# A sparse-attention and expert-attention kernel: half-size loads for batch 1, a converting load of the output weights, and a new order of all steps

## Chip, cores and metric

The kernel runs on one core of one Trainium2 chip. The metric is the device time of one execution in microseconds (us). The core has five engines that run their own queues in order: PE (matrix multiplications and transposes), DVE (vector), ACT (exponentials and copies), POOL (general, and the issuer of loads that convert types) and SP (issuer of plain loads and stores). They meet only at semaphores. The loads themselves are carried by 16 DMA engines.

## The reference

Two layers follow each other. The first is attention over q, k and v of 4 batches, 8 heads, 768 positions and 64 values: each query sees the keys closer than 16 positions, and beside them 24 summaries, one for each block of 32 positions (the maximum of its keys and the mean of its values).

```python
k_sum = k.reshape(B, H, nb, block, D).max(axis=3)
v_sum = v.reshape(B, H, nb, block, D).mean(axis=3)
scores_l = scale * q @ k.T            # kept where |i - j| < 16
scores_s = scale * q @ k_sum.T + log(block)
a = softmax(concat(scores_l, scores_s))
x = a @ concat(v, v_sum)              # heads side by side: 512 wide
```

The second is a mixture of four causal attention experts over x. A gate of four logits picks the best two experts of each position and weighs them by a softmax over the two; each expert has its own 512x64 matrices wq, wk, wv and a 64x512 matrix wo.

```python
for e in range(4):
    ye = causal_softmax((x@wq[e]) @ (x@wk[e]).T * scale) @ (x@wv[e]) @ wo[e]
    out += gate_weight[e] * ye        # zero where e is not among the two
```

## The kernel before

**Steps and the table.** The function `make_plan` defines 766 steps with `R.step`, and numbers them as they are defined. A step is a small piece of work for one engine, such as the 16 transposes that turn the keys of two heads. The text `TABLE` (lines 55 to 108) lists every step once as `number,engine,slots`: V is DVE, A is ACT, G is POOL, S is SP and P is PE; the slots say which buffer of its class each new tile takes. `Plan.emit` goes through it and calls the steps one by one. So each engine executes its steps strictly in the order of the table, and a step whose input is late holds up all that stands behind it on its engine.

**Names.** A step's name carries its batch, then its part. Heads go in pairs: `c` is 0 to 3, and two pairs form a group `g`. For batch 0, pair 1:

- `dk001`, `dq001` load keys and queries (lines 254 to 270; group 0, part 1). They are issued by POOL and convert fp32 to fp16 on the way. `load_qk` takes a number of parts: with 2 parts each load carries two heads, with 1 part four heads.
- `dv01` loads the values of the pair with four transfers on SP (lines 281 to 288), `hc01` copies the halo rows that neighbouring windows share (290 to 293), `bs01`, `be01` and `ds01` form the block means of the values (a product with the constant `sel`, an evacuation, a broadcast; 295 to 332). For the groups of batches 2 and 3 POOL adds up a tree instead (`dvs`, `tr`; 334 to 356).
- `tk01` and `tq01` transpose keys and queries on PE (372, 394). `tk` needs the constant `idr` (225), which is built from `id16`. `kw01`, `rk01`, `ksc01` and `cq01` evacuate them (376 to 401).
- `sc010`, `ex010`, `av010`: scores, exponential, product with the values, in two halves (406 to 442); they need the constants `mt` and `pi`. `rc`, `xm`, `tx`, `hi` and `lo` divide by the sum, transpose the result and split it into two fp16 parts (444 to 484).
- `weights` (486 to 537) loads the expert weights once, in fp32, into two spare `a2` buffers: `dw00` to `dw11` (wq and wk), `dwv0`, `dwv1`, `dwo`, all on SP. `cw`, `cvg` and `co` convert them to fp16.
- The second layer of a batch (539 to 751): `vp` (values and gate logits), `ga` to `gc` (gate), `pp` (projections), `sp` and `es` (scores and exponential of two experts, in six units), `dm` (causal mask on POOL), `aw` (products), `r2` and `wv` (weighting), `tw` and `ct` (transpose), `op` (product with wo, line 737), `oc` (evacuation) and `od` (store).
- `vone`, `id16`, `id32`, `idr`, `kwz`, `mt`, `pi`, `sel`, `knz`, `vtz`, `v2o`, `w1m`, `at`, `zz` build constants and clear paddings. `fl0` to `fl23` are products of a zero tile into unused banks; those marked P are executed, those marked A do nothing.

PE works on the second layer of one batch between the pieces of the first layer of the next. A single buffer `vt` serves the trees, six buffers `vb` the values, three each the keys and the queries, and seven rows `ob` the output.

**Order at the places that the prediction speaks of.** At the start POOL executes dk001, dk000, vone2, kwz, dq000, dq001, dq010, id16, idr, vone0, dq011, dk011, sel, ksc01, mt, hc00; ACT executes dwg, hc01, kw01, cq01, ds01, ex010, cq00, ksc00, ex011; PE executes tk01, bs01, tq01, tk00, tq00, sc010, bs00, sc011. Around the first use of wo PE executes sc200, tw000, sc201, sc211, tw010, pp101, sp115, sp114, tk22, tk23, sp111, op00, vp10.

The steps are executed by these lines, and the function whose loads change is this:

```python
for i, eng, slots in table:
    st = self.steps[i]
    ...
    st.fn(eng)
...
def load_qk(b, g, parts):
    n = 4 // parts
    ...
    R.step(f"dk{b}{g}{i}", {"G": 0.72}, [], [kn[b, g]], gk, dma=n * 96 * 0.098 / 16)
```

Of the kernel before, what the change touches and what calls it, by code (L numbers as in the profile page):

```python
# [15 lines left out]
S = 768  # L16
# [11 lines left out]
QP = 128  # L28
TREE = {(2, 0), (2, 1), (3, 0), (3, 1)}
# [31 lines left out]
233,G,2 252,P,6.1.1 83,V, 125,G, 111,P,4.4 84,V, 253,A, 0,G, 63,P,7.1 144,S,0 112,A, 128,P,0.5 64,V, 130,P,2.1 129,A,
143,S, 102,P,4.0.0 254,V, 131,A, 142,S,1 65,G, 113,P,0.0 269,P,7.0.2 103,V, 141,S, 132,P,2.0.2 270,A, 242,G,0 140,S,
104,V, 114,A, 145,S, 237,G, 271,V, 133,P, 85,P,4.1.1 235,G, 134,V, 135,V, 115,P,0.1.0 86,A, 116,P, 1,A, 87,V, 45,G,
136,P,6.2.2 117,V, 273,P,2.1 118,V, 137,A, 307,P,3.2 238,P,4.0 272,A, 138,V, 274,A, 150,G, 308,A, 275,P,0.2 239,V,
46,G, 119,P,6.3.3 276,A, 244,S,0 277,P,2.3 286,P,5.2.0 120,A, 240,G, 256,P,4.0 287,V, 278,A, 196,P,0.0 255,A, 241,G,
257,A, 288,V, 194,P,2.1 246,S,2 197,A, 121,V, 289,G, 149,G, 303,P,4.0.2 195,A, 290,P,5.1 304,V, 260,P,0.5 147,A,
204,P,6.0 408,S,0 279,P,2.0.1 406,S, 261,A, 305,V, 409,S, 280,P, 245,G, 205,A, 407,S, 152,P,0.0.0 402,S,3 281,V,
282,V, 291,A, 258,P,6.1 154,A, 283,P,4.4.4 259,A, 247,G, 153,V, 201,P,2 284,V, 202,A, 146,S, 306,G, 248,P,0.1 285,V,
401,G,1 203,G, 210,P,6 249,V, 198,P,2 263,P,4.1.2 199,A, 262,P, 251,G, 211,A, 165,P,0.2 404,S,4 264,V, 265,V, 415,G,2
213,P,2 292,P,6.4 410,G, 166,V, 214,A, 266,P,4.5.5 293,A, 311,P,2.0 267,V, 294,P,0.2 312,A, 158,P,6 295,A, 268,V,  # L70
400,G,1 309,P,2.3 250,G, 160,V, 207,P,0 310,A, 155,P,4 159,V, 208,A, 411,G,0 167,P,6.0 156,V, 157,V, 161,V,2.0 162,A,
163,V, 314,P,0.0.0 168,A, 313,P, 151,A, 164,V, 209,G, 585,S,0 172,P,4.1 200,G, 315,V, 169,P,6 582,S, 173,A, 316,V,
212,G, 297,P,2.1.1 584,S, 206,G, 583,S, 296,P, 170,A, 174,G, 413,G, 181,P,0 416,S,0 298,V, 317,P,4.6.6 299,V, 182,A,
449,P,6.0 432,P,7.1 318,V, 215,G, 450,A, 300,P,2.7.7 403,G, 178,P,0 433,A, 319,V, 445,P,6.1.1 418,S,5 179,A,
428,P,7.2.0 301,V, 184,P,4 414,G,1 185,A, 175,P,0 302,V, 364,P,4.1 183,G, 176,A, 171,G, 447,V, 180,G, 177,G, 362,P,2.0
365,A, 430,V, 186,G, 586,G, 446,A, 429,V, 216,P,0.0.0 218,P, 363,A, 188,P,1.1.4 217,P, 369,P,6.0 576,G,0 219,V,
375,P,2 448,A, 370,A, 189,P, 220,V, 431,G, 587,G,1 187,P, 376,A, 366,P,6 190,V, 323,P,0.1.1 367,A, 191,V, 434,P,2.5
324,V, 325,V, 192,P,4.0 436,P,6.1 435,A, 412,G, 193,V, 420,S,0 453,P,0.0 423,S, 221,P,2.1 454,A, 422,S, 335,P,4.2
222,V, 421,S, 437,A, 368,G, 578,S,2 377,G, 405,G, 381,P,0 372,P,2 336,V, 382,A, 462,P,6.0.2 373,A, 479,P,7.2.1 464,V,
378,P,0 223,P,4.0 379,A, 374,G, 320,P,2 480,A, 224,V, 380,G, 577,G,0 451,P,0.3 321,V, 383,G, 481,V, 225,S, 326,P,4  # L80
452,A, 419,G, 322,V, 463,A, 333,P,0.0 327,V, 371,G, 329,V,7.1 328,A, 424,G, 331,V, 330,A, 229,P,2.2 334,A, 332,V,
226,P,4.4 230,A, 590,G,1 346,P,0.1 227,V, 343,P,6 347,A, 386,P,1.0.2 425,G,0 384,P, 344,A, 228,S, 385,P, 337,P,4
387,V, 604,P,0.1.0 338,A, 388,V, 349,P,6 466,P,1.2 350,A, 606,V, 352,P,4 427,G, 456,P,2.0.2 597,S,0 353,A, 467,V,
340,P,6 389,P,4.0 341,A, 455,P, 390,V, 345,G, 348,G, 483,P,1.1 605,A, 592,S,4 354,G, 457,V, 439,P,4.1.0 458,V, 465,G,
351,G, 438,P, 484,A, 339,G, 38,G,1 482,A, 468,P,6.2 440,V, 470,P,2.4 441,V, 469,A, 625,P,0.0 621,P,1.0.2 471,A, 626,V,
342,G, 487,P,6.0 580,S,1 426,G, 459,P,4.0.0 488,A, 622,V, 485,P,2.3 608,P,0.2 486,A, 355,P,0.1.6 607,G, 623,V, 357,P,
609,A, 593,G, 594,S,3 356,P, 460,A, 612,P,2.1 358,V, 489,P,0.0.1 417,G, 359,V, 613,A, 490,P, 461,V, 588,G, 360,P,2.1
# [71 lines left out]
def make_plan(nc, T, q, k, v, moe_w_gate, moe_wq, moe_wk, moe_wv, moe_wo, out):  # L159
# [3 lines left out]
    def en(e):  # L163
        return getattr(nc, ENG[e])
# [109 lines left out]
    def load_v(b, c):  # L274
# [83 lines left out]
    def stage1_pair(b, c, hs, ls):  # L358
# [122 lines left out]
        def loc(e):  # L481
            nc.vector.tensor_tensor(turned(T["lo"][lo.slot]), xpv(),  # L482
                                    turned(T["hi"][hi.slot]), AL.subtract)
        R.step(f"lo{b}{c}", {"V": 0.96}, [xp, hi], [lo], loc)

    def weights():
        sA, sB = R.buf("a2"), R.buf("a2")
        wg32, wgt = st("wg32"), st("wgt")
        pw, pv, po = [st("pw0"), st("pw1")], st("pv"), st("po")
# [412 lines left out]
```

## Time and profile before

| what | value |
|---|---|
| time, median of 3 runs | 161.74 us (161.12 to 162.04) |
| time of the profiled execution | 162.94 us |
| span in its trace | 161.2 us |
| granted PE clock | 1.0 throughout |
| moved by DMA | 24.57 MB, mean 152 GB/s |
| read from and written to memory | 24.13 MB, 6.29 MB |

The page counts the busy time of each engine over the span, then cuts the span into 40 slices of 4.03 us, in which a digit is the busy share in tenths. A row of a timeline gives the start and the length of a run of like instructions, the engine, the line, the tiles (output, arrow, inputs) and, in brackets, how long the engine stood idle before it and what released it. Busy time of PE counts the length of instructions that overlap; two starts tell more than one length.

### The profile page before, as it was taken

How to read it: one execution, taken by the hardware profiler on the slowest of the kernel's cores; microseconds unless marked ns; L12 is line 12 of the kernel's file. 1: busy time of each engine (PE TensorE's matmuls, PEld its weight loads, DVE VectorE, ACT ScalarE, POOL GpSimd, SP SyncE). 2: the span in 40 equal slices, each digit the busy share in tenths (PEclk: the TensorE clock that was granted, in tenths of full speed). 3: DMA queues.
4: the chain of work that ended last, by engine and by line, in shares of the span. 5: the costliest groups of instructions: out<-in, count | busy, mean ns of one | idle time of the engine just before them, and what ended most of it. 6: DMA issues, size and time to landing. Idle time of an engine off the chain costs nothing.

```text
span 161.2 us, 6956 instructions
## 1 busy us (share of the span) xinstructions
PE 143.5 (89%) x2992; PEld 107.1 (66%) x2992; DVE 116.8 (72%) x236; ACT 119.5 (74%) x152; POOL 109.9 (68%) x184
## 2 busy tenths in 40 slices
PE   0049998769999999999999999998999998999994
PEld 0137796758687778577666988656778795466741
DVE  5527488985878967977786899968888578247940
ACT  0096999566996779898889997639788894999460
POOL 6987595984874999999999989649996230216100
PEclk9999999999999999999999999999999999999999
DMA  3999999997889996998799985699200000030746
GB/s 21 215 226 237 188 161 232 222 218 166 173 170 186 237 157 151 176 168 129 181 173 166 266 151 119 188 268 267 81 0 4 4 6 0 4 130 0 257 167 231
DMA packets 44158, 24.57 MB, mean 152 GB/s; under 512 B 33120, under 2 KB 40544, under 8 KB 43744
## 3 DMA queue, kind: packets, MB, share of 16 engines
q1 hardware_dynamic: 35552, 16.91, 43.7%
q0 software_dynamic: 7488, 6.29, 28.0%
q10 hardware_dynamic: 1088, 0.93, 1.7%
q8 instruction: 23, 0.38, 1.0%
q14 instruction: 7, 0.06, 0.1%
HBM read 24.13 MB, written 6.29 MB: 189 GB/s over the span
## 4 chain that ended last, share of the span: by engine, by line
PE 69%; ACT 12%; POOL 5%; issue 4%; DMA 4%; SPq 2%; DVE 2%; POOLq 0%; ACTq 0%; DVEq 0%
PE ps L437 13%; PE ps L630 12%; PE ps L554 6%; PE ps L678 6%; PE ps L654 6%; PE ps L366 6%; PE ps L737 4%; DMA out_dram<-ob 4%; PE ps L304 4%; PE ps L414 3%; PE ps L463 3%; ACT a L662 3%; PE ps L420 3%; ACT aT L427 2%; ACT kw L168 2%
## 5 line engine op out<-in xcount | busy, mean ns | idle before, releaser
L662 ACT ACTIVATE a<-ps 128x1024 f16<-128x1024 f32 (+1 forms) x48 | 41.7, 919 | 6.9 <-PE ps L654 4.9
L667 POOL TENSOR_SCALAR_AFFINE_SELECT a<-a 128x256 f16<-128x256 f16 x48 | 18.3, 406 | 22.1 <-ACT a L662 21.6
L427 ACT ACTIVATE aT<-ps 120x768 f32<-120x768 f32 x32 | 25.3, 812 | 4.5 <-PE ps L420 3.1
L437 PE MATMUL ps<-vb,aT 120*64 120x65 f32 x768 | 26.5, 224 | 1.3 <-issue 0.9
L437 PEld LDWEIGHTS ps<-vb,aT 120*64 120x64 f32 x768 | 24.1, 138 | 4.0 <-issue 2.4
L630 PE MATMUL ps<-hi,wqk 128*128 128x384 f16 x128 | 22.8, 326 | 0.3 <-ACT ob L168 0.3
L170 POOL COPY vb<-vb 32x1408 f32<-32x1408 f32 x15 | 20.1, 1350 | 3.7 <-DMA vb<-in_v_dram 3.1
L347 POOL TENSOR_TENSOR vt<-vt 120x1024 f32<-120x1024 f32 (+3 forms) x16 | 19.2, 1201 | 3.5 <-DMA vt<-in_v_dram 2.4
L630 PEld LDWEIGHTS <-wqk 128*128 128x128 f16 x128 | 11.7, 97 | 8.3 <-issue 1.0
L482 DVE TENSOR_TENSOR lo<-ps,hi 128x768 f16<-128x768 f32 x16 | 15.3, 955 | 1.3 <-ACT hi L168 0.8
L382 DVE TENSOR_REDUCE ks<-ps 128x24 f16<-128x768 f16 x16 | 15.0, 951 | 1.2 <-PE ps L366 1.0
L366 PE MATMUL ps<-idr,kn 100*64 100x100 f16 x256 | 8.9, 219 | 7.8 <-POOL idr L225 7.7
L452 DVE TENSOR_TENSOR x<-ps,rec 128x768 f32<-128x768 f32 x16 | 15.3, 958 | 0.6
L654 PE MATMUL ps<-qk,qk 64*128 64x512 f16 (+3 forms) x128 | 14.5, 307 | 0.7 <-ACT qk L168 0.4
L554 PE MATMUL ps<-wvg,hi 128*128 128x264 f16 x96 | 13.9, 276 | 0.1
L170 POOL COPY vb<-vu 24x768 f32<-24x768 f32 x16 | 13.1, 822 | 0.8
L366 PEld LDWEIGHTS <-kn 100*64 100x64 f16 x256 | 7.3, 117 | 9.0 <-DVE vb L210 5.6
L168 ACT COPY ob<-ps 128x1024 f32<-128x1024 f32 (+1 forms) x9 | 8.5, 968 | 6.1 <-PE ps L737 3.9
L170 POOL COPY vb<-vs 24x1536 f32<-24x1536 f32 x6 | 8.7, 1467 | 5.9 <-DVE vs L322 5.8
L678 PE MATMUL ps<-v,a 128*128 128x65 f16 x336 | 12.1, 193 | 0.0
L737 PE MATMUL ps<-wo,wT 128*128 128x512 f16 (+1 forms) x50 | 11.7, 371 | 0.4 <-DVE wT L170 0.4
L678 PEld LDWEIGHTS <-a 128*128 128x128 f16 x336 | 11.0, 97 | 1.5 <-issue 0.8
(95 smaller groups left out, 276.9 us busy)
## 6 DMA issues: line engine op xcount, KB each, us to landing
vb<-in_v_dram SPq DMA_DIRECT2D x32, 176.0 KB
out_dram<-ob SPq DMA_DIRECT2D x10, 512.0 KB
vt<-in_v_dram SPq DMA_DIRECT2D x16, 192.0 KB
kn<-in_k_dram POOLq DMA_DIRECT2D x6, 384.0 KB, 6.8
qn<-in_q_dram POOLq DMA_DIRECT2D x6, 384.0 KB, 6.6
kn<-in_k_dram POOLq DMA_DIRECT2D x4, 192.0 KB, 5.2
qn<-in_q_dram POOLq DMA_DIRECT2D x4, 192.0 KB, 5.9
a<-in_moe_wk_dram SPq DMA_DIRECT2D x2, 256.0 KB
```

The costliest lines, as they stand in the source:

```text
L170: en(e).tensor_copy(dst, src)
L347: en(e).tensor_tensor(y[0:120], x[0:120, 0:w], x[0:120, w:2 * w], AL.add)
L366: nc.tensor.transpose(dst[64 * hp:64 * hp + 64, p * s:p * s + p], src[:, hh + hp, 64 * s:64 * s + 64], idt)
L427: nc.scalar.activation(T["aT"][aT.slot][0:KR], pbank(sc, 2)[0:KR, :, 0:384], AF.Exp, scale=SCALE)
L437: nc.tensor.matmul(pbank(av, 2)[o:o + 64, u, 65 * (2 * (t // 2) + hp):65 * (2 * (t // 2) + hp) + 65], a[0:KR, hp, 64 * t:64 * t + 64], T[" ...
L554: nc.tensor.matmul(p[:, i, 0:264], hi_(ch)[:, cols], T["wvg"][:, ch, :], start=(ch == 0), stop=False, skip_group_check=True)
L630: nc.tensor.matmul(pbank(pp, 2)[:, u, 0:384], T["wqk"][:, cc, ch, j, :], hi_(ch)[:, 384 * u:384 * u + 384], start=(ch == 0), stop=(ch == N ...
L654: nc.tensor.matmul(pbank(sp, 2)[:, ep, c0:c0 + w], T["qk"][qk[1].slot][r, 128 * tj:128 * tj + 128], T["qk"][qk[0].slot][r, n0:n0 + w], sta ...
L662: nc.scalar.activation(a2v(u), pbank(sp, 2)[:, :, 0:ln], AF.Exp, scale=SCALE / (XS * XS))
L667: nc.gpsimd.affine_select(m, m, [[0, 2], [1, 128]], AL.is_ge, 0.0, base=0, channel_multiplier=-1)
L678: nc.tensor.matmul(pbank(av, 2)[:, ep, 65 * ti:65 * ti + 65], a2v(u)[:, ep, o:o + 128], T["v2"][v2.slot][:, tj, 2 * cc + ep, :], start=(tj ...
L737: nc.tensor.matmul(pbank(op, i1 - i0)[:, ti - i0, 0:n1 - n0], T["wT"][wTs[cc].slot][:, 128 * ti:128 * ti + 128], T["wo"][:, cc, n0:n1], st ...
```

## The change

The change has five parts.

1. The keys and queries of batch 1 come in loads of two heads each instead of four; that is four more load steps on POOL, with the same bytes in all.
2. The output weights are loaded by POOL straight into the fp16 tile `wo`, converted on the way. The fp32 load on SP and the conversion `co` are gone.
3. For the first pair loaded, (0, 1), the transfer of the last rows of values comes after the two large ones instead of ahead of them.
4. All 769 steps have a new order, new slots, and in part other engines. `idr`, `vone0`, `w1m` and `ds02` go from POOL to DVE; `hc00`, `hc03`, `ds13`, `ds22` and `ksc32` from POOL to ACT; `hc01`, `ds00`, `cvg`, `ksc10`, `ksc11`, `ksc23` and `ksc31` from ACT to POOL; `vone4` from DVE to POOL; `dwg`, `od32` and `od33` are issued by SP instead of ACT and `od31` by ACT instead of SP; fifteen evacuations move from DVE to ACT and eleven from ACT to DVE.
5. The planning figures of the changed steps (engine times and DMA times in the step definitions) are other ones; they have no effect on the emitted program.

The new order at the same places: at the start POOL executes dk001, id16, dk000, kwz, dq000, dq001, dk010, vone2, dk011, dq010, sel, hc01, cg, mt, ksc01, dq011, id32, dk100, dk101, ds00, dq110, dq100, ksc02, hc02, ksc03, dq101, ds03, hc10, dq111, ksc11, v2o, hc11; ACT executes kw01, kw00, cq01, cq00, hc00, ex010, ex011, hc03, ex001, kw02, ex000, cq02, cq03, kw03, ex020, ex030, ex031, hi00, ex021; PE executes tk00, tk01, bs01, tq01, tq00, sc011, sc010, sc001, bs00, tk02, av010, av011. Around the first use of wo PE executes sc200, vp11, tw000, sc211, tw010, sc201, sp114, sp115, op00, pp101, sp111, sc210, tk23, tk22, and POOL executes tr300, dm004, dq210, ksc20, tr301, dm110, dwo, vone1, hc21.

The core of the diff, with two rows of the new table:

```diff
+FIRST = (0, 1)
 ...
 TABLE = """
 ...
+139,S, 40,V,3 4,G,0 42,V,5 52,S,3 6,G, 2,G, 35,G, 3,G,0 8,V, 47,S,5 5,G, 57,G,1 7,V, 34,V, 71,P,0.0.0 39,G,2 59,G,
+66,S,2 37,V,0 88,P,1.1.1 58,G,1 89,A, 43,G, 53,G, 72,A, 90,V, 61,S,0 148,G, 54,P,2.0 73,V, 36,G, 92,P,3.0 55,V,
 ...
-            en(e).dma_start(out=w[32:80, :, 11, 0:64], in_=rows(0, 16 + 64 * 11, 48, S, 2))
+            def last():
+                en(e).dma_start(out=w[32:80, :, 11, 0:64], in_=rows(0, 16 + 64 * 11, 48, S, 2))
+
+            if (b, c) != FIRST:
+                last()
             for h in range(2):
                 en(e).dma_start(out=w[32:96, h, 0:11, 0:64], in_=rows(h, 16, 64, 64, 11))
+            if (b, c) == FIRST:
+                last()
 ...
         def dwo(e):
-            en(e).dma_start(out=f32(sB)[:, 1024:2048].rearrange("p (c n) -> p c n", c=2),
-                              in_=moe_wo.rearrange("(c e) d n -> (e d) c n", c=2))
-        R.step("dwo", {"S": 0.45}, [], [po], dwo, keep=[sB], dma=256 * 0.09 / 16)
+            nc.gpsimd.dma_start(out=T["wo"], in_=moe_wo.rearrange("(c e) d n -> (e d) c n", c=2))
+        R.step("dwo", {"G": 0.72}, [], [wo], dwo, dma=256 * 0.066 / 16)
 ...
-        def co(e):
-            copy(e, T["wo"].rearrange("p c n -> p (c n)"), f32(sB)[:, 1024:2048])
-        R.step("co", {"V": 0.68, "G": 1.04, "A": 1.0}, [po], [wo], co, keep=[sB])
 ...
-                load_qk(b, g, 2 if b == 0 else 1)
+                load_qk(b, g, 2 if b < 2 else 1)
```

More of the change, by code (lines that the diff above doesn't have):

```diff
@@ L61 @@
[L61 to L75, printed above, removed]
@@ new lines @@
+97,A, 105,P,4.2.2 50,V, 98,P,0.0.0 67,A, 99,P, 68,P,5.0 107,V, 51,G, 80,A, 235,S,3 100,V, 0,V, 101,V, 106,A,
+122,P,6.1.1 77,P,2.3 69,V, 102,P,0.0.0 244,G,0 78,A, 109,P,7.2 232,G,2 126,P,4.0 124,V, 110,A, 81,P,2.1.1 108,G,
+127,A, 103,V, 62,G, 82,P, 123,A, 111,P,4.4 104,V, 237,S,5 125,G, 63,P,7.1 112,A, 234,G, 83,V, 84,V, 128,P,0.5 70,G,
+130,P,4.1 129,A, 272,P,6.0.0 85,P,2.1.1 131,A, 236,G, 113,P,0.0 64,V, 144,S,0 274,V, 86,A, 132,P,4.0.2 143,S, 114,A,
+133,P, 246,G, 65,V, 142,S,1 273,A, 255,P,7.1.2 87,V, 275,G, 145,S, 276,P,0.1 46,G, 134,V, 257,V, 115,P,2.1.0 277,A,
@@ new lines @@
+292,G, 405,S,4 307,A, 197,P,6 252,V, 212,P,2 266,P,0.0.2 265,P, 149,G, 198,A, 403,G,0 407,S,5 164,P,4.2 213,A, 267,V,
+309,G, 1,A, 268,V, 253,G, 312,P,6.4 165,V, 297,P,2.0 313,A, 404,G,1 269,P,0.5.5 157,P,4 298,A, 413,G, 270,V, 254,A,
+154,P,6 158,V, 271,V, 159,A, 314,P,2.2 155,V, 156,V, 414,G,0 206,P,0 315,A, 295,P,4.3 166,P,6.0 207,A, 160,V,2.0
+162,V, 161,A, 316,P,0.1.0 167,A, 163,V, 317,P, 416,G, 587,S,0 296,A, 585,S, 168,P,6.0 586,S, 318,V, 171,P,2 588,S,
+169,A, 319,V, 299,P,4.0.1 415,G, 300,P, 172,A, 180,P,0 419,S,2 301,V, 320,P,6.6.6 208,G, 181,A, 302,V, 199,G,
@@ new lines @@
+452,P,2.0 214,G, 435,P,3.2 321,V, 453,A, 205,G, 177,P,4 303,P,0.7.7 211,G, 579,G,1 448,P,2.1.2 436,A, 322,V, 597,S,0
+178,A, 170,G, 431,P,3.0.1 202,G, 183,P,6 304,V, 173,G, 184,A, 174,P,4 417,G,0 449,A, 365,P,6.1 305,V, 179,G, 182,G,
+175,A, 433,V, 185,G, 367,P,0.0 589,G, 366,A, 450,V, 432,A, 215,P,0.0.4 368,V, 217,P, 421,S,3 451,A, 216,P, 176,G,
+372,P,6.1 218,V, 418,G,2 378,P,2 373,A, 186,P,1.1.0 434,G, 219,V, 188,P, 590,G,1 379,A, 187,P, 369,P,6 189,V,
+437,P,4.5 370,A, 190,V, 326,P,2.1.1 438,A, 191,P,6.0 327,V, 456,P,0.1 371,G, 328,A, 423,S,0 192,V, 220,P,4.1 146,G,
@@ new lines @@
+426,S, 457,A, 221,V, 439,P,2.4 424,S, 375,P,6 38,G,1 440,A, 384,P,4 425,S, 222,P,0.0 376,A, 338,P,2.2 223,V, 408,G,
+385,A, 381,P,6 339,A, 224,S, 454,P,4.2 374,G, 598,G, 482,P,0.2.0 465,P,1.0.2 382,A, 484,V, 329,P,2 455,A, 406,G,
+467,V, 323,P,6 483,A, 331,V, 380,G, 377,G, 330,V, 336,P,4.0 466,A, 324,V, 332,V,0.1 580,G,0 334,V, 333,A, 325,A,
+383,G, 228,P,2.2 386,G, 337,A, 335,V, 422,G, 225,P,6.4 229,A, 346,P,4.0 427,G, 226,V, 349,P,0 347,A, 387,P,1.0.2
+389,P, 350,A, 227,S, 352,P,6 230,S, 388,P, 353,A, 340,P,4 390,V, 485,G, 469,P,0.1 468,G, 391,V, 607,P,1.1.1 341,A,
@@ new lines @@
+459,P,6.1.2 428,G,0 470,V, 608,A, 392,P,2.0 458,P, 393,V, 355,P,4 609,V, 473,P,2.3 356,A, 486,P,0.2 474,A, 442,P,4.0.0
+460,V, 354,G, 461,V, 600,S,0 487,A, 348,G, 441,P, 601,S, 342,G, 430,G, 343,P,2 443,V, 471,P,0.0 344,A, 472,A, 444,V,
+628,P,6.0 624,P,7.0.0 629,V, 357,G, 490,P,4.1 610,G, 462,P,2.0.0 488,P,0.2 491,A, 345,G, 625,V, 351,G, 611,P,6.1
+489,A, 420,G, 360,P,0.1.4 612,A, 626,V, 358,P, 594,G,1 359,P, 463,A, 615,P,0.4 361,V, 592,G,1 493,P,6.1.1 616,A,
+362,V, 492,P, 429,A, 464,V, 627,G, 363,P,0.1 581,S,3 445,P,4.1.1 9,G, 364,V, 632,P,2.5 446,A, 593,G,2 494,V,
@@ new lines @@
+475,P,0.0.2 495,V, 633,A, 476,P, 447,V, 613,P,6.1 583,S, 496,P,2.2.2 477,V, 614,A, 478,V, 394,P,4.0 497,V, 400,P,6.4
+395,A, 498,V, 479,P,0.3.3 602,S, 397,P,4.2 480,A, 541,P,2.1 599,S, 401,A, 481,V, 398,A, 595,S,5 582,G, 543,P,6.0
+542,A, 591,G, 630,P,0.2 544,V, 645,P,4.2 631,A, 396,S, 641,P,5.2.2 646,V, 399,S, 551,P,2.1 584,G, 557,P,6 552,A,
+502,P,0.0.0 402,S, 558,A, 554,P,2 503,V, 643,V, 603,G, 658,P,4.1.1 504,A, 505,P,6 555,A, 660,V, 512,P,0.2 642,V,
+659,A, 604,G,0 507,A, 499,P,2 506,V, 545,P,4 500,V, 513,A, 548,P,6 501,V, 546,A, 617,P,0.1.0 508,V,2.0 559,G, 618,P,
@@ new lines @@
+672,P,2.7.7 530,G, 536,P, 673,A, 657,V, 690,P,6.1 537,V, 674,V, 688,P,4.0 691,A, 538,V, 568,P,2.0 569,V, 689,A,
+539,P,6.1 540,V, 692,P,0.1 707,P,4 695,P,2 708,A, 570,P,6.0 721,P,4.2 693,A, 709,G, 696,A, 571,V, 694,G, 701,P,0
+722,A, 572,S, 698,P,2 704,P,6 699,A, 723,P,4.0 702,A, 678,P,2.1.1 724,V, 705,A, 703,G, 700,G, 731,P,0.0 679,V, 680,V,
+728,P,4 732,A, 734,P,6 675,P,2 729,A, 733,G, 706,G, 681,P,0 735,A, 677,V, 676,V, 740,P,4 725,P,2 736,G, 682,V, 683,V,
+741,A, 576,P,6.2 726,A, 742,G, 684,V,4.1 697,G, 573,P,0.4 686,V, 685,A, 577,A, 727,G, 730,G, 687,V, 710,P,1.0.2 711,P,
@@ L108 @@
+574,A, 744,P,0.1.6 743,P, 713,V, 737,P,4 746,V, 575,S, 738,A, 714,V, 578,S, 747,V, 715,P,0.0 31,A,4 15,A,4 14,A,4
+11,A,4 716,A, 739,G, 748,P,4.1 712,P, 749,V, 13,A,0 28,A,0 32,A,0 757,P,0.0 717,V, 718,V, 745,P, 758,A, 754,P,4.4
+750,V, 759,A, 751,V, 719,P,2 26,A,0 755,A, 752,P,0 20,P,6 720,V, 27,P,7 753,V, 756,A, 763,P,2.6 16,A,3 29,A,3 24,A,3
+12,A,3 764,A, 760,P,6.2 25,A,7 765,S, 766,P,0.3 761,V, 21,P,1 23,P,4 767,V, 22,P,5 30,A,3 19,A,3 17,P,3 762,S, 768,S,
+33,P,7 18,P,2 10,P,1
 """
@@ L488, in weights @@
         wg32, wgt = st("wg32"), st("wgt")
-        pw, pv, po = [st("pw0"), st("pw1")], st("pv"), st("po")
+        pw, pv = [st("pw0"), st("pw1")], st("pv")
         def f32(bf):
```

48 lines of the change are left out of this document (11 added, 37 removed).

## The prediction

> **What bounds the kernel now.** I read the page first: the span, the busy shares, the 40 slices, the chain that ended last.
>
> ```profile
> span 161.2 us, 6956 instructions
> PE 143.5 (89%) x2992; PEld 107.1 (66%) x2992; DVE 116.8 (72%) x236; ACT 119.5 (74%) x152; POOL 109.9 (68%) x184
> PE   0049998769999999999999999998999998999994
> PE 69%; ACT 12%; POOL 5%; issue 4%; DMA 4%; SPq 2%; DVE 2%; POOLq 0%; ACTq 0%; DVEq 0%
> ```
>
> PE is the engine that the end hangs on: 69% of the chain, and nines from slice 9 on. What is not PE lies in the first eight slices. The view by stretches says how much.
>
> ```profile
> 20.00:30.00 10.00, 8.40 (x277) 7.22 (x269) 8.54 (x17) 9.47 (x11) 7.89 (x11) 1.00 1.13 195
> 50.00:60.00 10.00, 10.00 (x214) 7.73 (x208) 7.81 (x22) 7.58 (x11) 8.78 (x8) 1.00 1.14 208
> 70.00:80.00 10.00, 10.00 (x206) 7.07 (x203) 7.21 (x14) 8.67 (x12) 9.45 (x14) 1.00 0.85 151
> 100.00:110.00 10.00, 9.44 (x155) 6.10 (x150) 8.14 (x11) 5.89 (x8) 6.29 (x7) 1.00 0.84 223
> 140.00:150.00 10.00, 9.55 (x123) 6.46 (x118) 5.57 (x20) 9.49 (x13) 3.37 (x9) 1.00 0.15 58
> ```
>
> The columns after the length are PE, PEld, DVE, ACT, POOL, then clock, DMA share, GB/s. From 40 us on PE has no room; in 20 to 30 ACT (9.47) is the fullest and PE waits. Last the waits of PE, longest first:
>
> ```profile
> PE ps L366 <- POOL idr L225: 7.7, 1, 7.7
> PE ps L304 <- POOL sel L244: 2.2, 1, 2.2
> PE ps L366 <- issue: 1.3, 1, 1.3
> PE ps L437 <- issue: 0.9, 1, 0.9
> PE ps L414 <- ACT ob L168: 0.6, 1, 0.6
> ```
>
> The two large ones are waits for constants that POOL builds between its load issues, both over by 10.7 us. So a new order can win at the start, can win little after 40 us, and can lose anywhere by making PE, which executes in order, stand at a step whose input is late.
>
> **The change, part by part: the start.** These are the rows around PE's first work.
>
> ```profile
> 6.98 0.62 POOL L225 COPY idr<-id 100x2 f16<-100x2 f16 x3
> 7.55 0.13 POOL L210 MEMSET vb<- 96x24 f32 x1
> 8.40 0.09 POOL L214 MEMSET vb<- 16x2 f32 x1
> 7.66 0.88 PE L366 MATMUL ps<-idr,kn 100*64 100x100 f16 x16 [7.66 <-POOL idr L225]
> 10.46 0.18 POOL L244 TENSOR_SCALAR_AFFINE_SELECT sel<-sel 96x2 f32<-96x2 f32 x1
> 10.70 1.92 PE L304 MATMUL ps<-vb,sel 96*32 96x128 f32 x24 [2.16 <-POOL sel L244]
> ```
>
> In the new order id16 is POOL's second step and idr and vone0 go to DVE, so ahead of sel POOL has 0.62 us (idr) and 0.94 us (vone0, 7.55 to 8.49) less: sel ends at about 9.1 instead of 10.64, and bs01 starts 1.4 us earlier. The first transposes gain nothing: tk00 now comes first and needs dk000, issued third, so with a landing of 4.1 us or more they again start at 7 to 8. From there ACT carries the stage:
>
> ```profile
> 8.42 1.28 ACT L168 ACT_TABLE_LOAD   x1 [8.42 <-DMA vb<-in_v_dram]
> 9.71 1.36 ACT L168 COPY vb<-vb 32x1408 f32<-32x1408 f32 x1
> 10.98 1.10 ACT L168 COPY kw<-ps 128x1152 f16<-128x1152 f16 x1
> 13.45 0.80 ACT L168 COPY qT<-ps 128x768 f16<-128x768 f16 x1 [1.37 <-PE ps L366]
> 15.77 0.81 ACT L427 ACTIVATE aT<-ps 120x768 f32<-120x768 f32 x1
> 29.75 0.82 ACT L427 ACTIVATE aT<-ps 120x768 f32<-120x768 f32 x1
> 31.71 1.62 PE L437 MATMUL ps<-vb,aT 120*64 120x65 f32 x48
> 30.00 1.26 PE L437 MATMUL ps<-vb,aT 120*64 120x65 f32 x34 [0.88 <-issue]
> 36.08 1.65 PE L304 MATMUL ps<-vb,sel 96*32 96x128 f32 x48
> 30.00 2.65 POOL L170 COPY vb<-vb 32x1408 f32<-32x1408 f32 x2
> ```
>
> The last exponential of batch 0 (ex021) is the row at 29.75, ending 30.57, and the last PV product (av021) ends at 33.33. In the new queue ACT has, up to ex021, 4 kw copies of 1.10, 4 qT copies of 0.80, 2 halo copies (hc00, hc03) of 1.36, 8 exponentials of 0.81 and one hi copy, counted as a qT copy of the same 128x768: 17.6 us. With tk01 out at about 8.9 (two first transposes of 0.88 from 7.1 on) and the table load of 1.28 behind it, they run from 10.2 to 27.8 if ACT never waits. PE then has, beside work that fits earlier, av021 left and ends it at about 29.8, 3.5 us earlier than now. The 0.88 us "issue" pause in the present av031 is not a matter of order and may come again: 2.6. Further on, bs10 (36.08) needs the halo copies hc10 and hc11. Now they run at 30.00 to 32.65 on POOL; ended 1.4 us earlier, like sel, they would let bs10 start at about 31.3, 4.8 us earlier. But in the new order tx03 and tq13 (0.9 us, an estimate from the 0.90 for two transpose steps quoted below) are by then still to do, and the 1.3 us pause falls in this piece: 2.6 to 3.9. **Start: -3.0 us**; ends: 0 (loads in flight delay the inputs by as much as sel gains) and -4.8.
>
> The four extra load instructions of batch 1 cost POOL about 0.7 us each, 2.8 us. They lie between 15 and 30 us, where POOL is busy 7.89 of 10 and PE waits for ACT, so I cost them at nothing; without that cover hc11 and bs10 would be late by up to 2.8, which is the end at 0. The bytes are the same. What SP now does in another order (dwg first, v of pair 3 and 2 of batch 1 ahead of half the expert weights) I cost at nothing too: dwg's issue stands ahead of a wait for vone3 that is there anyway.
>
> **The output weights.** The ACT copy co goes (1.05 us at 59.4, in a stretch with ACT at 7.58 of 10): hidden, nothing. In its place the load itself must be in time, and it has been moved.
>
> ```profile
> L168 ACT CAST wo<-a x1: 1048/1048/1048, 59.4 to 59.4; 128x1024 f16<-128x1024 f32 x1
> 71.04 2.85 ACT L662 ACTIVATE a<-ps 128x1024 f16<-128x1024 f32 x3 [0.38 <-PE ps L654]
> 75.42 1.48 PE L630 MATMUL ps<-hi,wqk 128*128 128x384 f16 x8
> 77.20 0.90 PE L366 MATMUL ps<-idr,kn 100*64 100x100 f16 x32
> 78.03 0.39 PE L654 MATMUL ps<-qk,qk 64*128 64x256 f16 x4
> 78.36 1.04 PE L737 MATMUL ps<-wo,wT 128*128 128x512 f16 x4
> 77.08 0.76 POOL L667 TENSOR_SCALAR_AFFINE_SELECT a<-a 128x256 f16<-128x256 f16 x2
> kn<-in_k_dram POOLq DMA_DIRECT2D x4, 192.0 KB, 5.2
> DMA to landing us min/median/max: 4.1/6.1/7.2
> DMA to landing us min/median/max: 5.0/6.1/7.6
> ```
>
> dwo stands on POOL right behind dm110, which masks the output of es110, the third of the exponentials in the row at 71.04: it ends at 73.89. dm110 takes 0.41 (half of the two rows at 77.08, with the gap), so dwo issues at about 74.3 on the present clock, and not earlier; POOL's trees and masks ahead of it can only make it later. op00 now starts at 78.36; in the new order pp101 (75.42 to 76.83), tk22 and tk23 (77.20 to 78.03) and sp111 (0.33) stand behind it instead of ahead, so it is due at 75.8. Between are 1.5 us. A converting load issued by POOL landed 4.1 to 7.6 us after its issue (the last two rows: those of k and of q); the nearest in size are the two-head k loads, 192 KB against 256 KB written here, at 5.2. PE waits until 79.5: **+3.7 us**, ends +2.6 and +6.1. Behind op00 on PE stand pp101, the next scores and all the rest; ACT and DVE run dry behind it, while POOL goes on with hc21 and the masks.
>
> [...]
>
> **After that.** PE's rows are the same, so its time from op00 to the end is the present one less what it no longer waits for, since the other engines come out of the wait ahead. PE idles 0.56 us in 100 to 110 and 0.45 in 140 to 150; the 0.6 us wait for ob also goes with od02 issued ahead of the last v loads. I take **-1.0 us**, ends 0 and -1.5. The tail swaps SP and ACT as issuers of the last output loads: nothing, 0.4 either way.
>
> **Sum:** -3.0 + 3.7 - 1.0 = -0.3. The profiled execution took 162.94 us (span 161.2 and 1.7 around it), 0.7% above the median of 161.74; scaled, 162.6 becomes **161.4**.
>
> **Rivals.**
> (a) *wo is in time.* If the wait is 1 us or less (dm110 reached earlier, or PE held up elsewhere ahead of op00), the start is kept: -3.0 + 1 - 0.5, 159.2. For it: the start's gain is long, and PE may lose some of it before 75 us to new waits that hide the load. Against it: es110 feeds dwo and is tied to PE's own order, so both move together.
> (b) *Slower: the wait at op00 outgrows the start and cools PE.* It decides once the wait passes some 4.5 us, with landings near the 7.6 us end: wait 6.1, start 2.6, given back 1.0, and a PE that restarts slow. The trace has that: the 16 transposes at 7.66 took 0.88 us, while 16 of them took half of 0.90 in the row at 77.20. Some 4 us behind the wait at that rate would cost 2 us more: +2.5 to +4.5, so 164 to 166. [...]
> (c) *The start doesn't come.* DMA is full in 20 to 30 and 50 to 60 us (1.13 and 1.14 in the rows above); if hc11 or the first k load lands later in the new order, the start gives 0 to 1 us and the wait at op00 stays: +1.7 to +2.7, 163.5 to 164.4.
>
> **How the numbers follow.** The forecast as summed, 160.3 to 162.6: 0.42. (a) 0.24, (b) 0.17, (c) 0.17. Half a per cent, 0.8 us, is about what a measurement of this kernel can tell from no change. The forecast's share splits into 0.16 faster, 0.2 same and 0.06 slower; (a) is faster, (b) and (c) slower, but for 0.02 of (a) that is the same: **faster 0.38, same 0.22, slower 0.40**. The range reaches to (a) and over (c) to the foot of (b): 158.7 to 164.4.
>
> **What would show it.** bs01 should start near 9.2 instead of 10.70, av021 end near 30 and bs10 start near 32 to 33. The waits of PE should have a new line at L737, for the DMA into wo, of about 3.7 us; without it the sum fails on the fast side. The first matmul row behind it shows by its duration whether PE came back slow. If the first pass over batch 0 is not 2 us ahead, (c) holds. A new PE wait of over 1 us at another line would make the sum wrong in a way not named here.

## The result and the profile after

| | time, us |
|---|---|
| kernel before | 161.74 (161.12 to 163.69, 5 runs) |
| changed kernel | 172.65 (172.53 to 175.53, 5 runs) |
| ratio, 95% interval | 1.0682 (1.0641 to 1.0722) |
| forecast | 161.4 (158.7 to 164.4) |

The change made the kernel 6.8% slower. The forecast's middle was no change to be seen, and its range ended 8 us too early. Some executions of every kernel, the one before included, were lengthened by a disturbance; medians are of all runs, ratios leave those executions out.

The page of the changed kernel shows where the time is:

```profile
span 170.9 us, 6961 instructions
...
PE   0099999999999999910799998899999999899795
...
PEclk9999999999999999995579999999999999999999
...
PE 64%; DMA 11%; POOL 10%; DVE 6%; issue 3%; SPq 2%; ACT 2%; DVEq 0%; POOLq 0%; ACTq 0%
```

Counted from 0, PE is at nine tenths from slice 2 on, earlier than before (slice 9), but slices 17 and 18 are nearly empty, and in 18 and 19 the granted clock is at five tenths. DMA has risen from 4% to 11% of the chain. The waits of PE, longest first, name the load:

```profile
PE ps L740 <- DMA wo<-in_moe_wo_dram: 8.8, 1, 8.8
PE ps L374 <- DMA kn<-in_k_dram: 8.3, 1, 8.3
PE ps L718 <- DVE wav L707: 1.2, 2, 0.9
```

L740 is the product with wo, line 737 of the kernel before. The rows of PE around it:

```profile
73.14 0.47 PE L657 MATMUL ps<-qk,qk 64*128 64x512 f16 x4
82.38 1.89 PE L740 MATMUL ps<-wo,wT 128*128 128x512 f16 x4 [8.78 <-DMA wo<-in_moe_wo_dram]
84.06 2.77 PE L633 MATMUL ps<-hi,wqk 128*128 128x384 f16 x8
86.76 0.61 PE L657 MATMUL ps<-qk,qk 64*128 64x256 f16 x4
...
90.86 1.46 PE L633 MATMUL ps<-hi,wqk 128*128 128x384 f16 x8
```

PE stands from 73.6 to 82.38. Then the four products take 1.89 us, which took 1.04 before, and the eight projections 2.77, which take 1.46 again at 90.86: PE came back at half speed. On the other side stand POOL's and SP's issues and the time that wo took to land:

```profile
68.48 0.79 POOL L268 DMA_DIRECT2D qn<-in_q_dram  x1
...
72.97 0.73 POOL L520 DMA_DIRECT2D wo<-in_moe_wo_dram  x1
...
88.67 0.77 POOL L670 TENSOR_SCALAR_AFFINE_SELECT a<-a 128x256 f16<-128x256 f16 x2 [7.86 <-ACT a L665]
```

```profile
72.69 1.53 SPq L347 DMA_DIRECT2D vt<-in_v_dram  x4
```

```profile
DMA to landing us min/median/max: 9.4/9.4/9.4
```

The load was issued at 72.97, not late, and landed 9.4 us later. SP issued the four tree loads of batch 2, group 1 (`dvs210` to `dvs213`) from 72.69 to 74.22, beside it, and POOL had issued the query load `dq210` 4.5 us ahead of it. POOL's own later idle time of 7.86 us is PE's wait handed on through ACT.

The start, in comparison, came in part as forecast. These are bs01, av020 with av021 (one row), and bs10 of the changed kernel, then the first product of the experts (aw010) after and before:

```profile
9.73 0.64 PE L312 MATMUL ps<-vb,sel 96*32 96x128 f32 x2
...
30.50 1.62 PE L445 MATMUL ps<-vb,aT 120*64 120x65 f32 x48 [0.26 <-DVE lo L490]
...
32.50 1.53 PE L312 MATMUL ps<-vb,sel 96*32 96x128 f32 x48
...
66.64 1.44 PE L681 MATMUL ps<-v,a 128*128 128x65 f16 x42
```

```profile
68.91 1.68 PE L678 MATMUL ps<-v,a 128*128 128x65 f16 x50
```

At 66.64 against 68.91 the new order is 2.3 us ahead in this pair of profiles. Most of that need not be the order's own. PE has pauses that the profile puts under `issue`, which means that it waited for nothing that the profile shows: up to aw010 they take 0.88 and 1.26 us in the kernel before (the prediction shows both) and 0.30 us in the changed kernel, so they make 1.8 of the 2.3 us. In runs 6 and 7 below, which keep the old order, they take 1.4 and 1.0 us, and aw010 starts at 67.95 and 68.44.

So the account from span to span is: start -2.3, wait +8.8, slow restart +2.5 (the steps from op00 to pp100 took 8.48 us, and 5.98 in the run below that does not wait), and +0.7 left over behind it: 9.7, which is 170.9 less 161.2.

### The profile page after: what moved, and what is told of

It reads as the page before. It is cut to its first block, busy times and chain, and to the rows that moved or that the text cites. A ratio compares the mean times of both kernels' runs of the same rounds, so it can differ in the third digit from the quotient of the medians.

```text
span 170.9 us, 6961 instructions
## 1 busy us (share of the span) xinstructions
PE 147.0 (86%) x2993; PEld 107.9 (63%) x2993; DVE 113.6 (66%) x237; ACT 122.2 (72%) x154; POOL 111.1 (65%) x185
## 3 DMA queue, kind: packets, MB, share of 16 engines
HBM read 24.13 MB, written 6.29 MB: 178 GB/s over the span
## 4 chain that ended last, share of the span: by engine, by line
PE 64%; DMA 11%; POOL 10%; DVE 6%; issue 3%; SPq 2%; ACT 2%; DVEq 0%; POOLq 0%; ACTq 0%
PE ps L633 12%; PE ps L445 11%; PE ps L740 7%; PE ps L557 6%; DMA vb<-in_v_dram 6%; DMA wo<-in_moe_wo_dram 5%; PE ps L681 5%; PE ps L657 4%; PE ps L374 4%; PE ps L471 3%; PE ps L422 3%; POOL vt L355 3%; POOL a L670 3%; PE ps L312 2%; PE ps L428 2%
## 5 line engine op out<-in xcount | busy, mean ns | idle before, releaser
L172 POOL COPY vb<-vb 32x1408 f32<-32x1408 f32 x14 | 18.8, 1349 | 9.8 <-DMA vt<-in_v_dram 6.4
L633 PE MATMUL ps<-hi,wqk 128*128 128x384 f16 x128 | 24.4, 338 | 0.5 <-issue 0.3
L170 ACT COPY kw<-ps 128x1152 f16<-128x1152 f16 x13 | 14.5, 1134 | 8.4 <-PE ps L374 7.7
L740 PE MATMUL ps<-wo,wT 128*128 128x512 f16 (+1 forms) x50 | 12.7, 391 | 8.8 <-DMA wo<-in_moe_wo_dram 8.8
L633 PEld LDWEIGHTS <-wqk 128*128 128x128 f16 x128 | 12.4, 101 | 9.9 <-issue 2.8
L170 ACT CAST qk<-ps 128x768 f16<-128x768 f32 x10 | 8.1, 809 | 13.7 <-PE ps L633 13.7
L172 DVE COPY ob<-ps 128x1024 f32<-128x1024 f32 (+2 forms) x5 | 4.7, 957 | 13.7 <-PE ps L740 13.7
L740 PEld LDWEIGHTS <-wT 128*128 128x128 f16 x50 | 4.4, 100 | 13.9 <-DMA wo<-in_moe_wo_dram 8.9
L428 PEld LDWEIGHTS <-kw 64*128 64x128 f16 x384 | 10.5, 99 | 2.8 <-issue 0.7
```

Source lines behind the costliest of these rows:

```text
L170: nc.scalar.copy(dst, src)
L172: en(e).tensor_copy(dst, src)
L633: nc.tensor.matmul(pbank(pp, 2)[:, u, 0:384], T["wqk"][:, cc, ch, j, :], hi_(ch)[:, 384 * u:384 * u + 384], start=(ch == 0), stop=(ch == N ...
L740: nc.tensor.matmul(pbank(op, i1 - i0)[:, ti - i0, 0:n1 - n0], T["wT"][wTs[cc].slot][:, 128 * ti:128 * ti + 128], T["wo"][:, cc, n0:n1], st ...
```

## The experiments

The theory after the result: the new order itself is good, and all the loss comes from one step, the load of wo, which lands late because the query load and the tree loads share its way; PE's wait then brings a slow restart. Its rivals: the loss is spread over the order; a converting load is slow wherever it stands; the restart costs nothing of its own. The diffs give the order of steps on an engine, one name to a line, where no code is shown. In the quoted expectations e1 to e4 are runs 1 to 4, and e5 is run 8. Each ratio is to executions of the kernel before taken beside the run; a run of one execution has none.

**1. The wo load early**, behind `cw0` instead of behind `dm110`, all else as in the changed kernel.

```diff
 cw0
+dwo
 dk200
...
 dm110
-dwo
 vone1
```

> The changed kernel with one step moved: dwo, the converting load of the output weights, is issued by POOL behind cw0 (about 45 us) instead of behind dm110 (72.97 us). Theory A (the whole loss is PE standing 8.8 us for wo, and about 2.5 us more because PE comes back at a lower clock): the wait at the first product with wo goes, the clock stays at 1.0, and the time falls by about 11.3 us to 161 or a little under, since the start keeps its 2.3 us; 160 to 162. Theory B (the new order has a second bound behind the wait, such as POOL's trees or the last v loads, that the wait only hides): less than 8 us come back, 165 or more, and the place that gave way shows as a new wait of PE.

161.08 us (159.98 to 161.86, 4 runs); ratio to the kernel before 0.9896 (0.9807 to 0.9984). The wait and the slow restart are gone:

```profile
70.06 1.30 PE L681 MATMUL ps<-v,a 128*128 128x65 f16 x37 [1.34 <-POOL a L670]
...
74.88 1.04 PE L740 MATMUL ps<-wo,wT 128*128 128x512 f16 x4
...
80.86 1.46 PE L633 MATMUL ps<-hi,wqk 128*128 128x384 f16 x8
```

The last row is pp100. One instruction moved takes the span from 170.9 to 160.2, so the loss is not spread. What is left of the change is about 1% faster than the kernel before, with a wait of 1.34 us for a mask (`dm004`, which stands behind the tree sum `tr300` on POOL).

**2. PE kept busy through the wait.** 28 products of a zero tile into an unused bank go ahead of op00 (seven steps `fl` from the end of the table, six of which were marked A there).

```diff
 sp115
+fl0
+fl1
...
+fl6
 op00
```

> The changed kernel with seven idle products (28 matmuls of a zero tile into an unused bank, some 6 us of PE work) moved from the end of the table to just ahead of the first product with wo, so that PE works through most of the wait; the zero tile is cleared earlier, by DVE. The load of wo stays late. If the part of the loss behind the wait is PE's clock, the rows of op00 and pp101 return to 0.87 and 1.3 us, the granted clock to 1.0, and the time falls by 2.0 to 2.8 us, to about 170. If those rows were slow for another reason (loads under way, inputs late), the time stays within 0.7 us of 172.65 and they stay at twice their length.

169.23 us (168.13 to 171.07, 4 runs); ratio 1.0379 (1.0281 to 1.0477), against 1.0682 for the changed kernel.

```profile
75.15 6.20 PE L772 MATMUL ps<-zz 128*128 128x512 f16 x28 [0.62 <-ACT aT L435]
83.31 1.02 PE L740 MATMUL ps<-wo,wT 128*128 128x512 f16 x4 [1.95 <-DMA wo<-in_moe_wo_dram]
84.17 1.46 PE L633 MATMUL ps<-hi,wqk 128*128 128x384 f16 x8
...
89.27 1.46 PE L633 MATMUL ps<-hi,wqk 128*128 128x384 f16 x8
```

wo landed as late as before the edit (9.6 us), op00 even 0.9 us later, yet the projections run at 1.46 and pp100 (89.27) is 1.6 us ahead of the changed kernel's: 2.5 us are the price of the slow restart alone. By the ratios the time fell by some 3%, about 5 us, which is more than the 2 to 2.8 us expected; where the rest comes from no row here shows. With 6.20 us of products in the wait and stands of 0.62 and 1.95 us around them the granted clock stayed at 1.00 in run 2 (70 to 90 us); in the changed kernel, which stood 8.78 us there, it was 0.50 when PE came back.

**3. The query load behind the wo load** on POOL.

```diff
-dq210
 ksc20
 tr301
 dm110
 dwo
+dq210
```

> The changed kernel with dq210, a four-head query load that POOL issues 4.5 us ahead of dwo, moved behind dwo. Theory Q (wo is late because its packets queue behind those of dq210 on POOL's load queue, which ends only at 75.8): wo lands about 3 us earlier, 6 to 6.5 us after its issue instead of 9.4, and PE waits some 5.5 us. Theory S (wo is late because its packets share the 16 DMA engines with the four tree loads of 192 KB that SP issues at the same moment): the landing stays 8.5 to 9.5 us.

169.53 us (1 run); PE waited 4.9 us.

**4. The tree loads behind the first store** on SP:

```diff
-dvs210
-dvs213
-dvs211
-dvs212
 od00
+dvs210
+dvs213
+dvs212
+dvs211
```

> The changed kernel with the four tree loads dvs210 to dvs213 (192 KB each in rows of 8 KB), which SP issues at 72.7 to 74.2, moved behind the store od00, and so behind the first product with wo. Theory S: wo lands 5.5 to 7 us after its issue and PE waits some 5 us. Theory Q: the landing stays at 8.5 us or more, since dq210 is still ahead. If both share it, each of e3 and e4 takes a part off, 1 to 2.5 us.

169.39 us (1 run); PE waited 3.7 us. The landings, of run 3 and then of run 4:

```profile
DMA to landing us min/median/max: 6.2/6.2/6.2
```

```profile
DMA to landing us min/median/max: 4.7/4.7/4.7
```

Either company costs: without the query load ahead of it the landing falls from 9.4 to 6.2, as theory Q had it, and without the tree loads beside it to 4.7, less than theory S had it. Each takes off more than the 1 to 2.5 us expected if both share it. These are single executions; run 2, which left the company as it was, landed after 9.6, 0.2 from the changed kernel. The loads moved in run 4 are those of another queue, SP's; how they hold up a load of POOL's, no run here shows.

**5. Both at once.** The edit is that of run 3 and of run 4 together.

> The changed kernel with both hindrances of the wo load moved behind it at once: the query load dq210 behind dwo on POOL and the four tree loads dvs210 to dvs213 behind od00 on SP. One alone gave a landing of 6.2, the other 4.7, from 9.4. If the two hindrances act independently the landing falls to 4 us or less and PE's wait to 3.0 or less. If a load of this size simply needs about 4.7 us in this stretch, landing and wait stay at 4.7 and 3.7, and the time at 169 to 170.

168.29 us (1 run); the landing and PE's rows:

```profile
DMA to landing us min/median/max: 4.2/4.2/4.2
```

```profile
76.25 1.89 PE L740 MATMUL ps<-wo,wT 128*128 128x512 f16 x4 [2.48 <-DMA wo<-in_moe_wo_dram]
77.93 2.77 PE L633 MATMUL ps<-hi,wqk 128*128 128x384 f16 x8
...
85.04 1.46 PE L633 MATMUL ps<-hi,wqk 128*128 128x384 f16 x8
```

```profile
91.00 2.36 POOL L355 TENSOR_TENSOR vt<-vt 120x1024 f32<-120x1024 f32 x1 [6.29 <-DMA vt<-in_v_dram]
```

4.2 us is what the load took with both moved away: 0.5 less than without the tree loads alone, so without the tree loads the query load ahead matters little, and neither expectation is met exactly. The load came 0.9 us earlier as well (72.05, since POOL no longer spends 0.79 us on the issue of `dq210` first), so PE waited 2.5. The time fell little all the same, for two reasons. PE still restarted at half speed after a stand of 2.5 us (op00 to pp100 took 8.79). And the span is 4.3 us shorter than the changed kernel's while pp100 is 5.8 earlier: the tree loads put off came back as a loss later. POOL stands 6.29 us for their data, up to 91.00, and PE then waits behind POOL's later steps, 1.16 us the longest.

**6. The kernel before with a late converting load.** Its order stays; the fp32 load and `co` go, and the converting load stands behind `dm110`.

```diff
-        R.step("dwo", {"S": 0.45}, [], [po], dwo, keep=[sB], dma=256 * 0.09 / 16)
+        R.step("dwo", {"G": 0.72}, [], [wo], dwo, dma=256 * 0.066 / 16)
...
-        R.step("co", {"V": 0.68, "G": 1.04, "A": 1.0}, [po], [wo], co, keep=[sB])
```

> The kernel before, in its own order, with one part of the change: the converting load of wo in place of the fp32 load and the ACT copy, issued behind dm110 (77.5 us) as in the changed kernel. op00 is due at 78.4. [...] Theory B (the changed order as a whole is slower): no more than 2 us over the kernel before.

167.84 us (1 run); the landing was 5.6 us.

```profile
81.96 1.89 PE L733 MATMUL ps<-wo,wT 128*128 128x512 f16 x4 [4.50 <-DMA wo<-in_moe_wo_dram]
```

This one edit costs the old order about 5 to 6 us (161.74 in the first table, 163.07 for the kernel before taken beside this run), wait (4.50) and half-speed restart (1.89) alike, against at most 2 if the new order as a whole were at fault. Here the four tree loads were issued on SP up to 0.6 us before the load, and no query load stood just ahead of it on POOL; 5.6 is near run 3's 6.2.

**7. The same with the load early**, ahead of `hc13` (issued at 43.4).

```diff
 hc12
+dwo
 hc13
...
 dm110
-dwo
```

> The kernel before with the converting load of wo issued by POOL ahead of hc13 (about 45 us, in a pause of POOL) and without the fp32 load and the ACT copy of 1.05 us. The copy lies in a stretch in which ACT has room, so the time stays within 0.5% of the kernel before; the converting load by itself costs nothing. If it costs (POOL's issue of 0.73 us or its traffic) the time rises by up to 0.7 us.

162.78 us (161.84 to 166.71, 10 runs); ratio 1.0033 (0.9988 to 1.0079), no wait for wo. So a converting load with no conversion behind it is neither a loss nor a gain to be seen. It landed late here too (8.9 us), but nothing waited for it.

**8. The mask earlier as well.** Run 1 showed a wait for `dm004`. Here it goes ahead of `tr300`, and the wo load four steps further forward, ahead of `hc12`.

```diff
 hc13
+dwo
 hc12
...
+dm004
 tr300
-dm004
```

> The changed kernel with dwo issued ahead of hc12 (about 42 us, where POOL stands idle for a transfer of values) and the mask step dm004 moved ahead of tr300. In e1 the lead of 2.4 us at the scores fell to 1.1 us at a 1.3 us wait of PE for that mask, which stood behind a tree addition of 2.35 us on POOL. If that wait is a cost of its own, it goes and the lead stays at 2 us or more: 159.3 to 160.3, a ratio of about 0.988 to the kernel before. If PE is only held up elsewhere, the ratio stays at e1's 0.99 to 0.995.

161.81 us (159.62 to 166.78, 13 runs); ratio 0.991 (0.9854 to 0.9967).

**9. The mask alone**, with the load where run 1 had it:

```diff
+dm004
 tr300
-dm004
```

> The changed kernel with the wo load issued behind cw0, at about 48 us, as in e1, and the mask step dm004 ahead of the tree sum tr300 on POOL, which in e1 held the first product of the experts up for 1.3 us. If that wait was the rest of what the new order had lost, the end comes about 1 us earlier than in e1: 159.3 to 160.3, ratio 0.985 to 0.99 against the kernel before. If another step is late in its place, the time stays at that of e1.

161.05 us (159.7 to 164.67, 6 runs); ratio 0.9886 (0.9818 to 0.9953). In both profiles the wait for the mask is gone, and from aw010 to op00 run 9 takes 6.9 us against 8.4 in run 1. The time is that of run 1, so the gain of 1.3 us was not to be seen in it. The profiled executions took 166.78 and 164.67 us, 5.0 and 3.6 above the medians, and both hold a long pause of PE at the projections near 50 us; in run 9:

```profile
PE ps L633 <- issue: 3.3, 1, 3.3
```

The pause is not tied to these edits: the changed kernel has it too, at the same product, with 0.30 us, and runs 2 and 4, where nothing near 50 us was moved, with 1.1 and 1.2. What makes it long stays open; the last section says where such pauses come.

**10. The first keys at once.** To run 8, tk01 ahead of tk00, as in the kernel before.

```diff
+tk01
 tk00
-tk01
 bs01
```

> e5 with tk01 ahead of tk00 on PE. In the changed order the first transposes wait 8.1 us for dk000, the second key load, while dk001 landed at 5.3 us. If ACT's chain of copies and exponentials sets the first 30 us, as the prediction had it, ACT starts about 1.5 us earlier and av021 ends up to 1 us earlier than in e5. If PE's wait for the constant sel and the value loads (bs01 at 9.6) sets the stage, nothing changes within 0.3 us.

161.87 us (160.56 to 165.86, 12 runs); ratio 0.9957 (0.991 to 1.0004). tk01 starts 2.5 us earlier (6.3), but bs01 only 0.4 (9.19 against 9.56 in run 8). In the profile av020 and av021 come 1.0 us earlier than in run 8 (29.78 against 30.79), as the first of the two expectations had it, but only 0.4 earlier than in run 1. In the time no gain is to be seen.

**11. The constants alone.** To the kernel before: `id16` as POOL's second step, `idr` and `vone0` on DVE.

```diff
 dk001
+id16
 dk000
...
-id16
-idr
-vone0
```

> The kernel before with one edit at its start: id16 is POOL's second step, and idr and vone0 are built by DVE. If the constants set the start, as the prediction argued, bs01 starts about 1.4 us earlier than in the kernel before (10.7 to 9.3) and the time falls by 0.5 to 1.4, to 160.3 to 161.2. If the lead needs the new order of ACT and PE behind it, bs01 is early and the end is not: within 0.4 us of the kernel before.

162.34 us (161.15 to 170.79, 10 runs); ratio 0.9971 (0.991 to 1.0032). bs01 starts 1.6 us earlier, and then:

```profile
9.13 0.63 PE L304 MATMUL ps<-vb,sel 96*32 96x128 f32 x2 [1.94 <-POOL sel L244]
11.47 0.87 PE L304 MATMUL ps<-vb,sel 96*32 96x128 f32 x12 [1.71 <-ACT vb L168]
```

It stands 1.71 us for its halo rows, which ACT copies, and av021 starts 0.4 us later than before, not earlier. So the early constants alone give no lead there. From bs10 on this profile is 1.0 to 1.4 us ahead all the same: the `issue` pause of 1.26 us in front of bs10 is missing in it. Ten timed runs do not bear that lead out.

**12. Loads of four heads.** To run 1: keys and queries of batch 1 again in loads of four heads; all four extra load steps go, not three.

```diff
-                load_qk(b, g, 2 if b < 2 else 1)
+                load_qk(b, g, 2 if b == 0 else 1)
```

> The changed kernel with the wo load early (as in e1) and the keys and queries of batch 1 again in loads of four heads: three of the four extra load instructions are gone. If the halved loads cost or give nothing by themselves, as the prediction took, the steps up to the scores of batch 1 stand within 0.5 us of e1 and the time within 0.7 of it. If halved loads bring the lead of the start, the first steps of batch 1 (tk10 to bs10) come 1 to 2 us later than in e1 and the time rises to 162 or more. If the extra POOL issues had cost something, they come earlier.

163.46 us (161.82 to 166.36, 10 runs); ratio 1.0021 (0.9964 to 1.0079), its interval just above run 9's on the same chip. In the profile bs10 starts 2.2 us later than in run 1, but no product there waits for batch 1's keys. Instead PE runs at half clock in the first pass (granted 0.50 from 17.6 to 20.8 us) and has `issue` pauses of 1.2 and 0.7 us:

```profile
17.57 0.88 PE L373 MATMUL ps<-idr,kn 100*64 100x100 f16 x16
18.24 2.80 PE L444 MATMUL ps<-vb,aT 120*64 120x65 f32 x48
```

The same 48 products took 1.58 in run 1. So against run 9 the halved loads look to be worth about 1% in time, which the prediction had at nothing; against run 1 the intervals overlap (0.9964 to 1.0079 and 0.9807 to 0.9984). Nothing in the profile shows a way from the loads to the time, so this is not settled.

## Why the prediction was wrong

1. **What bounds the kernel, and "can lose anywhere by making PE stand at a step whose input is late":** right, and this is what happened.
2. **Start, -3.0:** near in size, in good part by luck. bs10 started at 32.50, in the forecast's 32 to 33, and aw010 was 2.3 us ahead. But bs01 came at 9.73 instead of 9.2, behind a wait for the first keys up to 8.25, and av021 ended at 32.12 instead of about 30, 1.2 us earlier than before instead of 2.6 or more. The forecast let ACT work from 10.2 to 27.8 without a wait and PE end av021 2.0 us later. In the trace ACT ended ex021 at 28.90, after waits of 2.7 us, and PE then still had tk10, tq11 and av020 ahead of av021, 3.2 us in all. Of bs10's 3.6 us of lead, 2.1 are the two `issue` pauses of the kernel before; nothing in the forecast says that the changed kernel would have none there. Constants off POOL, the other reason given, move bs01 and not av021 when nothing else is changed (run 11). The extra loads of batch 1, costed at nothing, may bring something (run 12). The new place of the first pair's last value rows (part 3) was not tried by itself.
3. **The wait at op00, +3.7 with ends 2.6 and 6.1: this step failed.** The mechanism, place and engine were as forecast; the size was not. The landing was taken at 5.2, the row nearest in bytes, with an upper end of 7.6; it was 9.4. The issue came 0.6 us before op00 was due instead of 1.5, which is the other 0.9 us of the difference. The rows from which the landing was taken belonged to other loads in other company, and what was in flight at 73 us in the new order was not asked: the new table, known beforehand, has dq210 ahead of dwo on POOL and dvs210 to dvs213 on SP at that place. Without them the load takes 4.2 (run 5). In the old order it took 5.6 at the same step (run 6), near the forecast, and where it was issued early 6.7 to 9.5 (runs 1, 7 to 10 and 12).
4. **Rival (b), the wait that cools PE:** this is the case that came, and its slow restart is shown by run 2 (eight projections in 1.46 us against 2.77). Its price of 2 us was near (2.5 us). Its range of 164 to 166 and its chance of 0.17 hung on a landing of at most 7.6 and so came out short.
5. **"Given back", -1.0:** did not come. From pp100 to the end the kernel before takes 79.2 us, the changed kernel 80.0 and run 1 79.3. The new order has waits of its own in place of those that were to vanish, such as:

```profile
160.34 0.29 PE L718 MATMUL ps<-id,wav 64*128 64x64 f16 x8 [0.85 <-DVE wav L707]
```

   This one, in the last batch, recurs to the hundredth in run 1 at 149.62: it belongs to the order and has nothing to do with wo.
6. **Conversion and load itself at nothing:** right (run 7, ratio 1.0033).

With the load early the same change is 1.0% faster than the kernel before (run 1; runs 8 and 9 alike). That is rival (a); its 159.2 was not reached, since the start gave 0.7 us less, the mask's wait of 1.3 was new and the 0.5 given back did not come.

## What to carry to other kernels

A load that is moved close to its use must be priced with what flies beside it at its new place, on its own queue and on the others (here a landing of 9.4 us, and 4.2 with both moved away); a landing read from a row elsewhere is no bound. Where an in-order engine waits for it, add the slow restart: it made the loss from an 8.8 us wait 11.3. When a large reordering comes out slow, move the one step at the longest wait first: here a single instruction held more than the whole loss, and the rest of the change was a gain of about 1%. A lead read from one pair of profiles must be cleared of the pauses that come and go (here 1.8 of 2.3 us).

## What the runs showed of the hardware

**A stand of 2.5 us halved the clock, and the slow stretches measured last about 3.4, 6.8 and 10.2 us.** The stretches of run 5 in which the granted clock changes (the column after the busy times):

```profile
75.20:75.40 0.20, 0.00 (x0) 0.00 (x0) 0.00 (x0) 0.20 (x2) 0.20 (x1) 1.00 1.38 219
75.40:75.60 0.20, 0.00 (x0) 0.00 (x0) 0.00 (x0) 0.14 (x1) 0.20 (x1) 0.55 1.24 189
...
82.00:82.20 0.20, 0.20 (x10) 0.20 (x8) 0.00 (x0) 0.20 (x1) 0.00 (x0) 0.50 0.78 174
82.20:82.40 0.20, 0.20 (x14) 0.20 (x12) 0.00 (x0) 0.20 (x2) 0.00 (x0) 0.88 1.25 414
```

and of the changed kernel:

```profile
77.20:77.40 0.20, 0.00 (x0) 0.00 (x0) 0.00 (x0) 0.00 (x0) 0.20 (x1) 0.92 0.41 82
77.40:77.60 0.20, 0.00 (x0) 0.00 (x0) 0.00 (x0) 0.00 (x0) 0.20 (x1) 0.50 1.06 190
...
87.40:87.60 0.20, 0.20 (x6) 0.12 (x4) 0.00 (x0) 0.20 (x2) 0.00 (x0) 0.50 1.09 420
87.60:87.80 0.20, 0.20 (x14) 0.16 (x10) 0.00 (x0) 0.20 (x2) 0.00 (x0) 0.98 0.95 369
```

In run 5 the clock fell at 75.4, 1.7 us into the stand, and stayed low for 6.8 us; in the changed kernel it fell at 77.4, 3.8 us into it, and stayed low for 10.2. Read the same way, runs 3, 4 and 6 (stands of 4.93, 3.72 and 4.50 us) show 6.8 each and run 12 3.4. In runs 8, 9 and 10 the mean clocks of 0.979, 0.990 and 0.990 over spans of 165.1, 163.0 and 162.7 us make about 6.9, 3.3 and 3.3 us at half clock, an estimate. What sets these lengths no run shows. In run 12 the clock fell at 17.5, after stands of 0.51 and 0.75 us; in run 2 a stand of 1.95 us did not bring it down. So no length of stand that is safe can be read from these runs. The price in the changed kernel is half of PE's time from its restart at 82.38 to the end of the slow stretch at 87.6, so 2.6 us, where 2.5 were measured. At the very start the column of the clock does not tell the speed: in the kernel before it reads 1.00 throughout, while 16 transposes took 0.88 us at 7.66 and 0.53 at 21.22.

**PE pauses that no release explains came at like counts of PE's products in different orders.** In the new order PE stops after the fifth of the eight products of pp000, near 50 us, in eight of ten profiles: for 0.2 to 1.2 us in the changed kernel and runs 2, 3, 4 and 12, and for 2.9 to 3.9 us in runs 8, 9 and 10, where the clock halved as well. The kernel before stops at other products, but run 12, in the new order, has its first two pauses at like counts. Here are the stretches up to the second pause of the kernel before and of run 12 (products of PE and weight loads of PEld in brackets):

```profile
0.00:35.80 35.80, 22.80 (x601) 19.13 (x602) 24.52 (x55) 22.97 (x27) 28.54 (x64) 1.00 1.11 191
```

```profile
0.00:35.40 35.40, 23.93 (x600) 19.84 (x600) 25.10 (x60) 21.36 (x24) 24.20 (x52) 0.95 1.03 174
```

The pauses before these come after 474 and 473 products, that at pp000 after 981 (the changed kernel and runs 9 and 12), and run 12 has one more after 1237. What PE waits for at these places the profile does not show, and no run tried it.
